# One-token decode block on one core: stationary values, 5p+k weights, wo by eight heads, feed-forward weights last

## The chip, the core and the metric

One NeuronCore of a Trainium2 chip runs the whole program. The metric is the device time of one execution in microseconds; the kernel before has a median of 693.3 us over three runs (693.24 to 693.9). A profile is one more execution, recorded instruction by instruction. In it PE is TensorE, PEld its weight loads, DVE VectorE, ACT ScalarE, POOL GpSimd, SP the engine that issues most transfers.

## The reference, cut to what matters

One token x of 640 features passes an attention block over a cache of 16,384 positions with 32 heads of 128, then a gated feed-forward of width 1,728. Both are modulated by six vectors made from c.

```python
mod = (silu(c) @ w_mod).reshape(1, 6, 1, 640)      # sa, ca, ga, sb, cb, gb
h = layernorm(x) * (1 + ca) + sa
q = (h @ wq) per head                              # 32 heads of 128
p = softmax(q . k_cache * 128 ** -0.5)             # 16384 scores a head
o = p . v_cache
x = x + ga * (o @ wo)
h = layernorm(x) * (1 + cb) + sb
x = x + gb * ((silu(h @ w_gate) * (h @ w_up)) @ w_down)
```

Everything is bf16. K and V are 32 x 4 MB each, 268 MB of the 290 MB that the core reads.

## The kernel before, in words

The kernel writes each engine's order out by hand. Every operation is given an engine, a position (a number that looks like a time in us) and the operations it depends on; each engine's operations are sorted by position (L91) and run in that order, waiting on semaphores. Positions are no delays: they only set the order on one engine. Nearly all transfers are issued by SP, whose order is therefore also the order of the transfers, and an SP issue that waits holds back all issues behind it.

**Layout.** In K and V a partition holds 128 consecutive positions, so that each partition's share of a head is one row of 32 KB. `kring` and `vring` hold two heads each. A vector of 640 features lies as 128 partitions by 5 columns with feature 128k+p in partition p, column k; c and x are read that way (L70), element by element. Weights follow: `(k p) n -> p k n`, so that a partition holds single rows of the matrix, and a stationary operand is a contiguous block of 128 columns.

**Start.** w_mod's first two vectors (L289), layernorm with two sums over partitions on GpSimd (L308, L316), then q for heads 0 to 3 (L338). The rest of wq takes the place of the first w_mod part and waits for it; its q products come later.

**A head.** ScalarE scales an identity by q (L402), PE multiplies it by ones so that q stands in every partition (L405), and ScalarE copies that to `qbc_sb` (L408). VectorE multiplies the whole K slot by q in place (L419), folds the 128 products of each position in halves: 128 to 64 out of the K slot into a buffer `f1` (L421), 64 to 32 and 32 to 16 in `f1` (L431), then sums 16 to one score (L433) and takes the maximum (L436). GpSimd takes the maximum over partitions (L439), ScalarE the exponential with its sum (L443), GpSimd the sum over partitions (L446). For values PE holds four columns of P stationary and streams V, 32 products of 512 columns (L458); the 4 x 512 result is copied (L464), its diagonal blocks are picked with eight small f32 matmuls (L470), scaled (L474), and multiplied at once by that head's 128 rows of wo (L481, five products).

**Loads of a head.** K(h) waits for the first fold of head h-2, V(h) for the value products of head h-2, the 160 KB of wo(h) for head h-2's wo products. On SP the order is K(h+1), V(h), wo(h-1) and so on. The last two V heads come in four pieces.

**End.** After V(31) SP loads the rest of w_mod into K slot 0, then w_gate, w_up and w_down into the weight region. The second layernorm (again two GpSimd sums) gives h; gate and up are one step of 140 products (L529) that waits for both weights; then the sigmoid and product on ScalarE and VectorE (L533 to L537), down in two steps, 60 and 10 products (L544), the gated residual (L549, L551), a transpose on PE (L553) and a copy (L554), so that the output is stored as five rows of 256 B.

Of the kernel before, what the change touches and what calls it, by code (L numbers as in the profile page):

```python
# [141 lines left out]
def build(nc, A_x, A_k, A_v, A_wq, A_wo, B_wg, B_wu, B_wd, c_in, w_mod, out, dbg=None, cfg=None):  # L142
    cfg = dict(cfg or {})
# [6 lines left out]
    FCH = (F + 127) // 128  # L150
    FLAST = F - 128 * (FCH - 1)
    NMOD = 6 * KC
    HB = min(cfg.get("HB", 4), H)
    assert H % HB == 0
    NQB = H // HB
    assert TT % 4 == 0
    NJ = TT // 4
    NFOLD = cfg.get("NFOLD", 3)
    SCALE = float(Dh) ** -0.5
    EPS = 1e-5  # L160
    PERIOD = 20.0
    T0 = 21.0
    NKP0 = 4 if TT % 16 == 0 else 1
    def NVP(h):
        return 4 if (h >= H - 2 and TT % 16 == 0) else 1

    es = ExitStack()
    with es:
        block = es.enter_context(nc.Block())
        plan = _Plan(nc, es)  # L170
        if cfg.get("names") is not None:
            plan.names = cfg["names"]

        def sb(name, shape, dtype):
            return es.enter_context(nc.sbuf_tensor(name, list(shape), dtype))

        ones_bf = sb("ones_bf", [128, 128], BF16)
        ident = sb("ident", [128, 128], BF16)
        c_col = sb("c_col", [128, KC], BF16)
        x_col = sb("x_col", [128, KC], BF16)  # L180
        LATE_MB = (TT * 128 >= KC * 4 * D) and H >= 3
        NA = 2 * KC
        WMA_E = KC * 2 * D
        WQ0_E = KC * HB * 128
        WQR_E = KC * (H - HB) * 128
        WMB_E = KC * 4 * D
        FFN_E = 2 * KC * F + FCH * D
        WREG_E = max(WMA_E + WQ0_E, WQR_E, FFN_E) + (0 if LATE_MB else WMB_E)
        wreg = sb("wreg", [128, WREG_E], BF16)
        wma_v = wreg[:, 0:WMA_E].rearrange("p (k n) -> p k n", k=KC)  # L190
        wq0_v = wreg[:, WMA_E:WMA_E + WQ0_E].rearrange("p (k n) -> p k n", k=KC)
        wqr_v = wreg[:, 0:WQR_E].rearrange("p (k n) -> p k n", k=KC) if H > HB else None
# [4 lines left out]
        if LATE_MB:  # L197
            wmb_v = kring[:, (H - 2) % 2].rearrange("p t d -> p (t d)")[:, 0:WMB_E].rearrange("p (k n) -> p k n", k=KC)
        else:
            wmb_v = wreg[:, WREG_E - WMB_E:WREG_E].rearrange("p (k n) -> p k n", k=KC)  # L200
        vring = sb("vring", [128, 2, TT, 128], BF16)
        f1 = sb("f1", [128, TT, 64], BF16)
        woring = sb("woring", [128, 2, D], BF16)
        S_sb = sb("S_sb", [128, 2, TT], F32)
        P_sb = sb("P_sb", [128, 2, TT], BF16)
        R_sb = sb("R_sb", [128, 2, 128], BF16)
        qbc_sb = sb("qbc_sb", [128, 2, 128], BF16)
        q_bf = sb("q_bf", [128, H], BF16)
        q_r32 = sb("q_r32", [128, H], F32)
# [7 lines left out]
        On = sb("On", [128, H], BF16)  # L217
        acc_sb = sb("acc_sb", [4, 2, 512], F32)
        onesf = sb("onesf", [4, 4], F32)
        identf = sb("identf", [4, 4], F32)  # L220
        mod_col = sb("mod_col", [128, NMOD], F32)
        onep = sb("onep", [128, 2, KC], F32)
# [5 lines left out]
        st = sb("st", [128, 16], F32)  # L228
        xc = sb("xc", [128, KC], F32)
        junk = sb("junk", [128, KC], F32)  # L230
# [5 lines left out]
        tt2 = sb("tt2", [128, KC], F32)  # L236
        h2_col = sb("h2_col", [128, KC], BF16)
# [5 lines left out]
        tt3 = sb("tt3", [128, KC], F32)  # L243
        o_col = sb("o_col", [128, KC], BF16)
        o_row = sb("o_row", [KC, 128], BF16)

        psb = [es.enter_context(nc.psum_tensor("psb%d" % i, [128, 512], F32)) for i in range(8)]
        qbc_ps = [psb[0][:, 0:128], psb[1][:, 0:128]]
# [3 lines left out]
        q_ps = psb[5]  # L252
        g_ps = psb[4]
        u_ps = psb[5]
        f_ps = psb[6]
        oT_ps = psb[7]
        acc_ps = [psb[6][0:4, :], psb[7][0:4, :]]
# [3 lines left out]

        o_ones = op(POOL, 0.0, lambda e: e.memset(ones_bf[:], 1.0), name="ones")
        o_ident = op(POOL, 0.1, lambda e: e.affine_select(
            out=ident[:], in_=ones_bf[:], pattern=[[1, 128]], compare_op=ALU.is_equal,
            fill=0.0, base=0, channel_multiplier=-1), deps=[o_ones], name="ident")

        o_onesf = op(POOL, 0.2, lambda e: e.memset(onesf[:], 1.0), name="onesf")
        o_identf = op(POOL, 0.3, lambda e: e.affine_select(
            out=identf[:], in_=onesf[:], pattern=[[1, 4]], compare_op=ALU.is_equal,
            fill=0.0, base=0, channel_multiplier=-1), deps=[o_onesf], name="identf")  # L270

        wm_src = w_mod.rearrange("(k p) n -> p k n", p=128)
        d_wm = plan.dma(0.0, wma_v, wm_src[:, :, 0:2 * D], "wm", name="dma_wmod_a")
        d_c = plan.dma(0.1, c_col[:], c_in[0].rearrange("(c p) -> p c", p=128), "c", noncontig=True, name="dma_c")
        d_x = plan.dma(0.15, x_col[:], A_x[0, 0].rearrange("(c p) -> p c", p=128), "x", noncontig=True, name="dma_x")
        wq_src = A_wq.rearrange("(k p) n -> p k n", p=128)
        d_wq0 = plan.dma(0.3, wq0_v, wq_src[:, :, 0:HB * 128], "wq0", name="dma_wq0")

        o_tbl = op(ACT, 0.0, lambda e: e.preload_act_table_set("natural_log_exp_and_others"), name="tbl")
# [5 lines left out]
        def f_mod(e, wv, j0, j1, jofs):  # L285
            last = None
            for j in range(j0, j1):
                for k in range(KC):
                    last = e.matmul(mod_ps[:, j:j + 1], lhsT=wv[:, k, 128 * (j - jofs):128 * (j - jofs + 1)], rhs=silu_c[:, k:k + 1],  # L289
                                    start=(k == 0), stop=(k == KC - 1))  # L290
            return last
        o_mod = op(PE, 1.0, lambda e: f_mod(e, wma_v, 0, NA, 0), deps=[d_wm, o_sc], name="mod_mm_a")
        o_modc_a = op(ACT, 1.5, lambda e: e.activation(out=mod_col[:, 0:NA], in_=mod_ps[:, 0:NA], func=ACTF.Copy), deps=[o_mod], name="mod_col_a")
        TLAST = T0 + (H - 1) * PERIOD
        if LATE_MB:
            TB = TLAST + 2.0
            TBC = TLAST + 41.5
        else:
            TB = T0 + 2 * PERIOD - 4.0
            TBC = min(TB + 2.5 * PERIOD, T0 + H * PERIOD - 8.0)  # L300
        mb_deps = [o_sc, o_modc_a]
        d_wm_b = None
        o_onep = op(DVE, 1.6, lambda e: e.tensor_scalar_add(out=onep[:, 0, :], in0=mod_col[:, KC:2 * KC], scalar1=1.0), deps=[o_modc_a], name="onep_a")
        o_onep_b_pos = TBC + 0.4

        def layernorm_ops(pos, src_f32, src_dep, rs_col, tag, xc_t, want_rs=None):
            c0 = rs_col
            o_tot = op(POOL, pos, lambda e: e.partition_all_reduce(  # L308
                st[:, c0 + 1:c0 + 2], st[:, c0:c0 + 1], channels=128, reduce_op=bass.bass_isa.ReduceOp.add),
                deps=[want_rs], name=tag + "_tot")  # L310
            o_xc = op(DVE, pos + 0.1, lambda e: e.tensor_scalar(
                out=xc_t[:], in0=src_f32[:], scalar1=float(D), scalar2=st[:, c0 + 1:c0 + 2], op0=ALU.mult, op1=ALU.subtract),
                deps=[o_tot, src_dep], name=tag + "_xc")
            o_sq = op(ACT, pos + 0.2, lambda e: e.activation(
                out=junk[:], in_=xc_t[:], func=ACTF.Square, accum_out=st[:, c0 + 2:c0 + 3]), deps=[o_xc], name=tag + "_sq")
            o_tot2 = op(POOL, pos + 0.3, lambda e: e.partition_all_reduce(  # L316
                st[:, c0 + 3:c0 + 4], st[:, c0 + 2:c0 + 3], channels=128, reduce_op=bass.bass_isa.ReduceOp.add),
                deps=[o_sq], name=tag + "_tot2")
            o_ln = op(ACT, pos + 0.4, lambda e: e.activation(
                out=st[:, c0 + 4:c0 + 5], in_=st[:, c0 + 3:c0 + 4], func=ACTF.Ln, scale=1.0 / float(D) ** 3, bias=EPS),  # L320
                deps=[o_tot2], name=tag + "_ln")
            o_rstd = op(ACT, pos + 0.5, lambda e: e.activation(
                out=st[:, c0 + 5:c0 + 6], in_=st[:, c0 + 4:c0 + 5], func=ACTF.Exp, scale=-0.5, bias=-math.log(float(D))),
                deps=[o_ln], name=tag + "_rstd")
            return o_xc, o_rstd

        o_xf = op(ACT, 0.3, lambda e: e.activation(out=x_f32[:], in_=x_col[:], func=ACTF.Copy, accum_out=st[:, 0:1]), deps=[d_x], name="x_f32")
        o_xc, o_rstd = layernorm_ops(0.6, x_f32, o_xf, 0, "ln1", xc, want_rs=o_xf)
        o_t1 = op(DVE, 1.7, lambda e: e.scalar_tensor_tensor(
            out=tt1[:], in0=xc[:], scalar=st[:, 5:6], in1=onep[:, 0, :], op0=ALU.mult, op1=ALU.mult),  # L330
            deps=[o_xc, o_rstd, o_onep], name="t1")
        o_h = op(DVE, 1.8, lambda e: e.tensor_tensor(out=h_col[:], in0=tt1[:], in1=mod_col[:, 0:KC], op=ALU.add), deps=[o_t1, o_modc_a], name="h_col")

        def f_q(e, wv, h0, h1):
            last = None
            for hh in range(h0, h1):
                for k in range(KC):
                    last = e.matmul(q_ps[:, hh:hh + 1], lhsT=wv[:, k, 128 * (hh - h0):128 * (hh - h0 + 1)], rhs=h_col[:, k:k + 1],  # L338
                                    start=(k == 0), stop=(k == KC - 1))
            return last  # L340
# [10 lines left out]
        if H > HB:  # L351
# [3 lines left out]
            for hh in range(HB, H):  # L355
                o_qr[hh] = o_qr1
# [272 lines left out]
```

## Time and profile before

| What | Value |
|---|---|
| median of the runs | 693.3 us (693.24 to 693.9) |
| profiled execution, first to last instruction (its span, and the only time recorded of it) | 692.7 us |
| busy: PE, DVE, ACT, POOL | 358.9, 618.7, 82.9, 255.5 us |
| bytes read | 290.47 MB, 419 GB/s over the span |
| packets of transfers | 22,176, of which 9,610 under 2 KB and 3,146 under 512 B |
| chain that ended last | DMA 62%, DVE 32%, issue 3% |
| first K multiply starts | 23.67 us |
| K load, issue to landing, median | 26.6 us |

The page cuts the span into 40 slices of 17.3 us and shows the busy share of each engine and of the 16 transfer engines in tenths. A group line gives line, engine, operation, shapes and count, then busy time, mean ns of one, idle time before it and what ended that. A row of the stretches gives the stretch, its length, the busy time and count of each engine, the granted TensorE clock, the share of the transfer engines and the rate. The chain is followed back from the last instruction: each step was released by the one before it.

### The profile page before, as it was taken

The numbers are of one execution on the slowest core, as the hardware profiler recorded it, in microseconds if no ns is written. First come the engines' busy times: TensorE is split into PE (matmuls) and PEld (weight loads), VectorE is DVE, ScalarE is ACT, GpSimd is POOL, SyncE is SP. The second block draws the span as 40 slices with busy tenths as digits, with TensorE's granted clock in tenths as the row PEclk, the third lists the DMA queues.
The fourth block names the chain that finished last, engine by engine and source line by source line (L and its number), as shares of the span: only waits on it lengthen the run. The fifth ranks groups of instructions, "written<-read, shape, count | busy, mean of one in ns | idle before, by whom it ended". The sixth has DMA issues, their size and how long they took to land.

```text
span 692.7 us, 4851 instructions
## 1 busy us (share of the span) xinstructions
PE 358.9 (52%) x1993; PEld 152.9 (22%) x1993; DVE 618.7 (89%) x220; ACT 82.9 (12%) x309; POOL 255.5 (37%) x76
## 2 busy tenths in 40 slices
PE   0025655444666544446555444566554446655665
PEld 0022212112222211122221212222121122221225
DVE  0699999999999999999999999899999999999911
ACT  1101101111011011111110111101011111110110
POOL 0043334444433344443334444023344443334400
PEclk9999767777666777766777776666677776677985
DMA  8999999999999999999999999999999999999995
GB/s 296 426 441 425 430 431 429 430 430 427 425 436 431 430 428 429 433 428 431 431 428 425 432 433 428 427 433 433 425 430 428 431 431 430 431 431 414 419 408 211
DMA packets 22176, 290.79 MB, mean 420 GB/s; under 512 B 3146, under 2 KB 9610, under 8 KB 12810
## 3 DMA queue, kind: packets, MB, share of 16 engines
q1 hardware_dynamic: 22154, 290.48, 98.9%
q8 instruction: 15, 0.25, 0.1%
q14 instruction: 7, 0.06, 0.0%
HBM read 290.47 MB, written 0.00 MB: 419 GB/s over the span
## 4 chain that ended last, share of the span: by engine, by line
DMA 62%; DVE 32%; issue 3%; SPq 1%; PE 1%; ACT 0%; POOL 0%; POOLq 0%; DVEq 0%
DMA kring<-in_A_k_cache_dram 58%; DVE kring L419 20%; DVE f L421 10%; DMA wreg<-in_B_w_up_dram 4%; SPq L71 1%; PE psb L529 1%; DVE f L431 1%; PE psb L544 0%; DVE S_sb L433 0%; PE psb L338 0%; ACT P_sb L443 0%; POOL st L308 0%; ACT R_sb L402 0%; POOL st L316 0%; POOL gm L439 0%
## 5 line engine op out<-in xcount | busy, mean ns | idle before, releaser
L458 PE MATMUL psb<-vring,P_sb 128*4 128x512 bf16 x1024 | 293.1, 456 | 10.6 <-DMA vring<-in_A_v_cache_dram 9.7
L419 DVE TENSOR_TENSOR kring<-kring,qbc_sb 128x16384 bf16<-128x16384 bf16 (+1 forms) x35 | 278.6, 7959 | 19.1 <-DMA kring<-in_A_k_cache_dram 16.6
L446 POOL PARTITION_ALL_REDUCE Ls<-rs x32 | 233.5, 7295 | 34.8 <-ACT P_sb L443 34.8
L439 POOL PARTITION_ALL_REDUCE gm<-pm x32 | 19.6, 612 | 354.8 <-DVE pm L436 344.2
L421 DVE TENSOR_TENSOR f<-kring 128x8192 bf16<-128x8192 bf16 (+1 forms) x35 | 142.1, 4059 | 1.2
L458 PEld LDWEIGHTS psb<-vring,P_sb 128*4 128x4 bf16 x1024 | 97.1, 98 | 194.0 <-issue 96.6
L405 PE MATMUL psb<-R_sb,ones_bf 128*128 128x128 bf16 x32 | 9.2, 288 | 235.8 <-ACT R_sb L402 235.8
L431 DVE TENSOR_TENSOR f<-f 128x4096 bf16<-128x4096 bf16 x64 | 112.5, 1758 | 2.2
L433 DVE TENSOR_REDUCE S_sb<-f 128x128 f32<-128x2048 bf16 x32 | 73.1, 2286 | 1.1
L405 PEld LDWEIGHTS psb<-R_sb,ones_bf 128*128 128x128 bf16 x32 | 3.3, 104 | 238.7 <-ACT R_sb L402 238.7
L464 ACT ACTIVATE acc_sb<-psb 4x512 f32<-4x512 f32 x32 | 18.8, 586 | 284.7 <-PE psb L458 284.7
L470 PE MATMUL psb<-identf,acc_sb 4*128 4x1 f32 x256 | 33.5, 248 | 21.6 <-ACT acc_sb L464 21.6
L470 PEld LDWEIGHTS psb<-identf,acc_sb 4*128 4x128 f32 x256 | 30.8, 186 | 37.8 <-ACT acc_sb L464 37.8
L448 ACT ACTIVATE lnl<-Ls 128x1 f32<-128x1 f32 x32 | 6.5, 203 | 221.7 <-POOL Ls L446 221.7
L338 PE MATMUL psb<-h_col,wreg 128*128 128x1 bf16 x160 | 4.6, 165 | 28.6 <-DMA wreg<-in_A_wq_dram 18.0
L481 PE MATMUL psb<-On,woring 128*128 128x1 bf16 x160 | 8.9, 166 | 19.7 <-ACT On L474 19.7
L491 DVE TENSOR_SCALAR onep<-mod_col 128x5 f32<-128x5 f32 x1 | 0.2, 169 | 16.2 <-ACT mod_col L490 16.2
L443 ACT ACTIVATE P_sb<-S_sb,nb 128x128 bf16<-128x128 f32 x32 | 12.9, 402 | 1.0
L402 ACT ACTIVATE R_sb<-ident,q_r 128x128 bf16<-128x128 bf16 x32 | 12.4, 387 | 0.0
L481 PEld LDWEIGHTS psb<-On,woring 128*128 128x128 bf16 x160 | 6.1, 97 | 22.4 <-ACT On L474 22.4
L338 PEld LDWEIGHTS psb<-h_col,wreg 128*128 128x128 bf16 x160 | 4.4, 104 | 28.8 <-DMA wreg<-in_A_wq_dram 18.2
L408 ACT ACTIVATE qbc_sb<-psb 128x128 bf16<-128x128 f32 x32 | 8.9, 277 | 12.2 <-PE psb L405 12.2
(61 smaller groups left out, 70.7 us busy)
## 6 DMA issues: line engine op xcount, KB each, us to landing
kring<-in_A_k_cache_dram SPq DMA_DIRECT2D x31, 4096.0 KB, 26.6
vring<-in_A_v_cache_dram SPq DMA_DIRECT2D x30, 4096.0 KB, 30.4
vring<-in_A_v_cache_dram SPq DMA_DIRECT2D x8, 1024.0 KB, 22.1
woring<-in_A_wo_dram SPq DMA_DIRECT2D x32, 160.0 KB, 28.4
wreg<-in_A_wq_dram SPq DMA_DIRECT2D x1, 4480.0 KB, 20.1
kring<-in_A_k_cache_dram SPq DMA_DIRECT2D x4, 1024.0 KB, 10.3
kring<-in_w_mod_dram SPq DMA_DIRECT2D x1, 3200.0 KB, 27.1
wreg<-in_B_w_gate_dram SPq DMA_DIRECT2D x1, 2160.0 KB, 31.9
```

The source lines that it names most:

```text
L405: o_qbcmm[h] = op(PE, base - 14.8 if h > 0 else 2.7, lambda e, s2=s2: e.matmul(qbc_ps[s2], lhsT=ones_bf[:], rhs=R_sb[:, s2], start=True, s ...
L419: o_m = op(DVE, base + 3.3 * c, lambda e, ksl=ksl, qb=qb: e.tensor_tensor(out=ksl, in0=ksl, in1=qb, op=ALU.mult), deps=[d_k[h][c], o_qbc[h ...
L421: o_f = op(DVE, base + 3.3 * c + 2.2 + (6.6 if npc == 1 else 0.0), lambda e, ksl=ksl, c=c, KP=KP: e.tensor_tensor(out=f1[:, c * KP:(c + 1) ...
L431: prev = op(DVE, base + 13.3 + i, lambda e, w=w: e.tensor_tensor(out=f1[:, :, 0:w], in0=f1[:, :, 0:w], in1=f1[:, :, w:2 * w], op=ALU.add), ...
L433: o_red[h] = op(DVE, base + 17.0, lambda e, w=w, s2=s2: e.tensor_reduce(out=S_sb[:, s2], in_=f1[:, :, 0:w], axis=AX.X, op=ALU.add), deps=[ ...
L439: o_gm[h] = op(POOL, base + 19.6, lambda e, h=h: e.partition_all_reduce(gm[:, h:h + 1], pm[:, h:h + 1], channels=128, reduce_op=bass.bass_ ...
L443: o_exp[h] = op(ACT, base + 20.4, lambda e, h=h, s2=s2: e.activation(out=P_sb[:, s2], in_=S_sb[:, s2], func=ACTF.Exp, scale=SCALE, bias=nb ...
L446: o_L[h] = op(POOL, base + 21.0, lambda e, h=h: e.partition_all_reduce(Ls[:, h:h + 1], rs[:, h:h + 1], channels=128, reduce_op=bass.bass_i ...
L458: last = e.matmul(acc_ps[s2], lhsT=P_sb[:, s2, 4 * j:4 * j + 4], rhs=vring[:, s2, 4 * j:4 * j + 4, :].rearrange("p a d -> p (a d)"), start ...
L464: o_acc[h] = op(ACT, base + 39.5, lambda e, s2=s2: e.activation(out=acc_sb[:, s2, :], in_=acc_ps[s2], func=ACTF.Copy), deps=[o_pvlast[h], ...
L470: last = e.matmul(OT_ps[:, h:h + 1], lhsT=acc_sb[:, s2, 128 * i:128 * (i + 1)], rhs=identf[:, i:i + 1], start=(i == 0), stop=(i == 3))
L481: last = e.matmul(attn_ps[:, cc:cc + 1], lhsT=woring[:, s2, 128 * cc:128 * (cc + 1)], rhs=On[:, h:h + 1], start=(h == 0 and cc == 0), stop ...
```

## The change

It is a rewrite of most of `build`; the planner is the same.

- **Feature 5p+k.** Partition p, column k now hold feature 5p+k. Every weight is read `(p k) n -> p k n`, so that a partition holds five consecutive rows, and c, x and the output are 10 contiguous bytes a partition. Stationary operands then step through the matrix: by 5 elements in w_mod, wo and w_down, by 13 in gate and up (feature 13p+k of the 1,664 that fill 13 columns; the last 64 are as before). The transpose at the end goes.
- **c and x** are issued by ScalarE, ahead of its table load; all others by SP.
- **Sums over partitions** of the layernorms are PE products with f32 ones instead of GpSimd reductions. GpSimd has one warm-up reduction.
- **q** is broadcast by the matmul itself: h is the stationary operand, its column repeated 128 times, and wq is streamed, 512 columns at a time. `qbc` keeps all heads. wq has a place of its own.
- **Folds in place.** `f1` goes: all folds write into the K slot, which becomes free at the reduction (L422 of the new kernel) instead of the first fold. K(h+1) is issued ahead of V(h), as it was.
- **Values stationary.** Each 128 x 128 block of V is loaded as weights and multiplied by one column of P, 128 products a head, which gives the output as a column; no diagonal.
- **wo by eight heads.** wo is read in four loads of 1.3 MB, eight consecutive rows a partition (10,240 B). The eight head outputs are put through a masked copy and one small matmul to the layout that this needs, then 40 products.
- **The end.** V(30) whole, the rest of w_mod, V(31) in halves, then w_gate, w_up and w_down in three pieces. Gate and up are two steps that wait for their own weights; down has three.

SP's order is now: w_mod's first part, wq of heads 0 to 3, K(0) in quarters, K(1), V(0), the rest of wq, wo, K(2), V(1), K(3), V(2), and so on.

```diff
-            d_wo[h] = plan.dma(base + 1.5, woring[:, s2], A_wo[h * 128:(h + 1) * 128, :], ("wo", s2),
+            if h % GW == 0:
+                d_wo[g8] = plan.dma(base + 13.0, wo_sb[:], A_wo[g8 * GW * 128:(g8 + 1) * GW * 128, :].rearrange("(p k) n -> p k n", p=128),
+                                    "wo", deps=[o_wo[g8 - 1]] if g8 else [], name="dma_wo%d" % g8)
...
-            kdeps = [o_fold1[h - 2]] if h >= 2 else []
+            deps = [o_red[h - 2]] if h >= 2 else []
...
+        d_c = plan.dma(0.0, c_col[:], c_in[0].rearrange("(p k) -> p k", p=128), "c", name="dma_c", eng="act")
...
+            o_tot = op(PE, pos, lambda e: e.matmul(st_ps[:, c0:c0 + 1], lhsT=ones_f[:], rhs=sum_ap, start=True, stop=True),
...
+                        last = e.matmul(mod_ps[:, m * KC + k:m * KC + k + 1],
+                                        lhsT=wv[:, kd, (m - m0) * D + k:(m - m0 + 1) * D:KC], rhs=silu_c[:, kd:kd + 1],
...
+                    last = e.matmul(q_ps[b][:, 0:n * 128], lhsT=h_col[:, k:k + 1].broadcast_to([128, 128]),
+                                    rhs=wv[:, k, n0:n0 + n * 128], start=(k == 0), stop=(k == KC - 1))
...
-                    out=f1[:, c * KP:(c + 1) * KP, :], in0=ksl[:, :, 0:64], in1=ksl[:, :, 64:128], op=ALU.add),
+                    out=ksl[:, :, 0:64], in0=ksl[:, :, 0:64], in1=ksl[:, :, 64:128], op=ALU.add),
...
-                        last = e.matmul(acc_ps[s2], lhsT=P_sb[:, s2, 4 * j:4 * j + 4],
-                                        rhs=vring[:, s2, 4 * j:4 * j + 4, :].rearrange("p a d -> p (a d)"),
+                        last = e.matmul(OT_ps[:, h:h + 1], lhsT=vring[:, s2, t, :], rhs=P_sb[:, s2, t:t + 1],
+                                        start=(t == 0), stop=(t == TT - 1))
...
+                out=Z[:, zb, JW * hl:JW * (hl + 1)], in_=msk[:], func=ACTF.Copy, scale=on_f[:, h:h + 1]),
+                o_am[g8] = op(PE, base + 29.4, lambda e, zb=zb: e.matmul(A_ps[:, 0:GW], lhsT=Z[:, zb], rhs=e8[:], start=True, stop=True),
+                            last = e.matmul(attn_ps[:, cc:cc + 1], lhsT=wo_sb[:, k, cc:D:KC], rhs=A_sb[:, zb, k:k + 1],
...
+                        last = e.matmul(ps_t[:, j:j + 1], lhsT=wv[:, k, j:128 * NF:NF], rhs=h2_col[:, k:k + 1],
+        o_g = op(PE, TE + 1.2, lambda e: f_gu(e, wg_v, g_ps), deps=[o_h2, d_wg, o_zg], name="gate")
+        o_u = op(PE, TE + 1.25, lambda e: f_gu(e, wu_v, u_ps), deps=[o_h2, d_wu, o_zu], name="up")
+                        last = e.matmul(f_ps[:, cc:cc + 1], lhsT=wd_v[0:kw, k, cc:D:KC], rhs=gu_col[0:kw, k:k + 1],
```

## The prediction

> **What bounds the kernel now.** I read the page's 40 slices first, then the costliest groups, then busy time by stretch, and last the chain that ended last.
>
> ```profile
> DMA  8999999999999999999999999999999999999995
> GB/s 296 426 441 425 430 431 429 430 430 427 425 436 431 430 428 429 433 428 431 431 428 425 432 433 428 427 433 433 425 430 428 431 431 430 431 431 414 419 408 211
> ```
>
> The transfers are busy in every slice. 290 MB go by at about 430 GB/s; only the first slice (296) and the last four (414, 419, 408, 211) fall below. So time can be won at the two ends, or by bytes that move faster, and hardly by less compute in the middle. The second limit is close:
>
> ```profile
> L419 DVE TENSOR_TENSOR kring<-kring,qbc_sb 128x16384 bf16<-128x16384 bf16 (+1 forms) x35 | 278.6, 7959 | 19.1 <-DMA kring<-in_A_k_cache_dram 16.6
> ...
> L421 DVE TENSOR_TENSOR f<-kring 128x8192 bf16<-128x8192 bf16 (+1 forms) x35 | 142.1, 4059 | 1.2
> ...
> L431 DVE TENSOR_TENSOR f<-f 128x4096 bf16<-128x4096 bf16 x64 | 112.5, 1758 | 2.2
> L433 DVE TENSOR_REDUCE S_sb<-f 128x128 f32<-128x2048 bf16 x32 | 73.1, 2286 | 1.1
> ```
>
> By the groups with shapes kept apart, VectorE's head is 8.69 + 4.42 + 2.29 + 1.23 + 2.29 + 0.29 = 19.2 us, 19.4 with handovers (621.70 to 641.08 in the timeline). Multiplies start 19.9 us apart (601.82, 621.70, 641.61), with 0.5 us of waiting for K. A head moves 8.55 MB, 19.9 us at 430. Transfers set the pace and VectorE follows half a microsecond behind.
>
> The stretches show the ends (us; busy time and count of PE, PEld, DVE, ACT, POOL; granted clock; DMA share; GB/s):
>
> ```profile
> 7.00:8.00 1.00, 0.00 (x0) 0.00 (x0) 0.00 (x0) 0.00 (x0) 0.00 (x0) 1.00 0.41 14
> 8.00:9.00 1.00, 0.00 (x0) 0.00 (x0) 0.36 (x2) 0.21 (x1) 0.00 (x0) 1.00 0.34 37
> 400.00:500.00 100.00, 54.51 (x224) 21.48 (x223) 95.14 (x31) 12.16 (x45) 34.31 (x10) 0.68 1.01 430
> 670.00:678.00 8.00, 5.83 (x122) 4.34 (x121) 0.48 (x5) 1.11 (x4) 0.12 (x1) 0.87 1.03 405
> 680.00:683.00 3.00, 1.62 (x61) 1.65 (x62) 0.31 (x2) 0.00 (x0) 0.00 (x0) 0.50 1.06 363
> 686.00:687.00 1.00, 0.05 (x1) 0.05 (x2) 0.76 (x4) 0.00 (x0) 0.00 (x0) 0.50 0.16 55
> 687.00:688.00 1.00, 1.00 (x39) 1.00 (x40) 0.00 (x0) 0.00 (x0) 0.00 (x0) 0.50 0.00 0
> ```
>
> From 7 to 9 us the share is 0.41 and 0.34 and only 51 KB move: that is where c and x come in 1,280 pieces of 2 bytes. At 670 to 678 (gate and up, rows of 3,456 B) a full share yields 405 GB/s, at 680 to 683 (w_down, rows of 1,280 B) 363. The last bytes land near 686.5. What follows is in the chain:
>
> ```profile
> 681.38 4.42 PE psb L529 x140
> ...
> 686.95 1.77 PE psb L544 x60
> 688.73 0.05 issue
> 688.77 1.25 PE psb L544 x10
> ...
> 690.77 0.27 ACT o_row L554
> ```
>
> All 140 gate and up products wait for w_up (landed 681.24), so down begins at 686.95, after the bytes are in: 6.2 us from the last byte to the span's end.
>
> **The change, part by part.** The sum is made against the span, 692.7 us; the median of the runs is 693.3, so I add 0.6 at the end.
>
> *Transfers.* Bytes stay, pieces grow. (1) c and x: 256 pieces of 10 B on ScalarE's queue beside w_mod. The hole is 2.0 us long for 0.1 us of work; a fifth of the pieces takes a fifth of its busy share (0.75 us): 0.2. Won: 1.7. (2) wo: 5.24 MB in rows of 1,280 B, priced by w_down's row (363): 14.4 us; in 10,240 B pieces near 425: 12.3. I take 2.0, with 0 as the lower bound, since no row has wo alone. (3) gate and up: 4.42 MB, 10.9 us at 405 against 10.3 at 428: 0.6. (4) w_down: 2.21 MB, 6.1 against 5.3 (most pieces 11,520 and 5,120 B): 0.8. (5) V(30) whole and V(31) in halves instead of quarters: 417 GB/s from 641 to 661 against 430, 8.4 MB: 0.5. Sum 5.6: the last byte lands at 680.9.
>
> [...]
>
> *The last bytes.* Gate now waits for w_gate alone, up for w_up, and w_down is three steps, the last of 64 rows. After the last byte come 5 products of 64 rows (0.18 each in the by-form groups, 0.9), two VectorE steps (0.4 with handovers), the store (691.04 to 692.7: 1.66; transpose and copy, 0.6 us, go, 128 pieces instead of 5 may cost 0.2): 3.1 instead of 6.2. Won: 3.1.
>
> *Is TensorE then late?* V(31) now comes after w_mod's second part, and the feed-forward weights (6.6 MB, 15.5 us) after that; its last half lands near 665. Then: 64 value products 2.0 (31 ns each, as gate's 140 in 4.40); head output, masked copy, small matmul, copy and 40 wo products 2.4; residual 0.65 (L507 to L510); layernorm 2.9 (677.61 to 680.35 today, two GpSimd sums of 0.38 become f32 matmuls of about 0.5 by L470's 0.19 load and 0.25 product); gate and up 4.4; gu 0.2; down 2.9; end 2.2. Sum 17.6: 682.6 on this path against 680.9 + 3.1 = 684.0 on the transfers'. Slack 1.4.
>
> *Strided weights.* With feature 5p+k, the stationary operands of w_mod, wo and w_down step by 5 elements and those of gate and up by 13. The trace has no such load. Bounds: nothing (contiguous bf16, 31 ns a pair) and 100 ns more, the f32 load of L470 (8 pairs in 1.05 us, 131 ns). The nearest row, same type and size, is the contiguous one; I take nothing, keep both ends. On the path stand 250 of them (40 + 140 + 70): each extra ns is 0.25 us, the first 5 ns are free.
>
> [...]
>
> *Values stationary.* 128 pairs of 31 ns, 4.0 us a head for 9.2 (L458, 293.1 over 32), and the 4-row copy and diagonal products go. PE was not the bound: nothing, except that V slots free earlier.
>
> *K slot freed later.* K(h+2) now waits for the reduction instead of the first fold: 2.29 + 1.23 + 2.29 and handovers, 5.9 us later; the order K(h+1), V(h) on SP stays. Cover: K lands 26.6 us after issue, 9.7 of them its own, so 17 us stand ahead; 11 remain. Cost nothing; with the cover gone each us late is lost per head. The V load queued behind it on SP waits no longer than K.
>
> *In-place folds.* Same counts; only the row pitch is 256 B instead of 128. L419 and L431 are in place already. Nothing; bounds are in the rivals. Without wo a head's transfers take 8.39 MB / 431 = 19.5 us against VectorE's 19.4, so VectorE nearly ties, with 11 us of queue as buffer.
>
> *Start.* Sums move from GpSimd (its first waits until 18.53) to PE, and the first multiply from 23.67 to about 12.5, when K(0)'s first quarter lands. Nothing won: K(1), V(0), wq, wo fill the queue to about 51, and K(2), free at 32, is late next. The seven q evictions stand on ScalarE ahead of head 1's exp and wait for wq (about 50); only head 1's value product and V(3) wait for that, 20 us later.
>
> Sum: 692.7 − 5.6 − 3.1 = 684.0, plus 0.6: **684.6 us**.
>
> **Rivals.** *Slow strided loads, slower side.* One mechanism: PE's 250 loads after V(31). At L470's 100 ns extra: 682.6 + 25 = 707.6, 708.2 as a median. It decides beyond 5 ns and loses to before beyond (692.7 − 682.6) / 0.25 = 40 ns. For: 2-byte steps break the contiguous pattern of every load seen. Against: same type and size as the 31 ns rows. *Half rate*, 27 ns more on all: 689.4, 690.0 as a median; on gate and up alone 687. *Pieces bring nothing*: if 363 and 405 come from the queue running out, only the tail is won: 692.7 − 3.1 + 0.6 = 690.2. For: the share falls to 0.16 at the very end. Against: 670 to 678 is mid-queue at 1.03. *VectorE becomes the bound*: if the 256 B pitch costs the folds and reduction 10% (1.0 us of 10.2), 32 us build up, less 11 of queue, 21 on 684.6: 706. Against: L431's 32-element runs already run at L421's rate.
>
> **How the numbers follow.** Forecast 0.50 (681 to 686.5); half rate 0.18 (686 to 692); pieces bring nothing 0.12 (688 to 691.5); slow loads over 40 ns 0.12; VectorE 0.05; near no change 0.03. Two tenths of a percent (1.4 us) is about what a measurement here can tell. Faster 0.50 + 0.17 + 0.12 = 0.79, same 0.04, slower 0.17. The range 681 to 692 holds the first three, 0.80; its lower end has the engines' uneven finish (share 0.64 to 0.16, about 2 us) gone, its upper end the half rate.
>
> **What would show it.** After: no stretch below 0.9 of DMA share from 3 us to the end; wo's heads no slower than others; last byte near 681; a chain that ends with w_down's landing and ten or fewer products. Gate's 70 products should take 2.2 us; 5 or more means strided loads cost. I am wrong if the chain's end is PE, or VectorE waits for nothing between heads.

## The result and the profile after

The changed kernel takes 698.0 us (median of four runs, 697.32 to 699.3) against 693.27 (four runs, 693.17 to 693.9). The ratio is 1.0067, with an interval of 1.0053 to 1.0082: slower by 4.7 us, where 684.6 was predicted and 681 to 692 given as the range. The profiled execution took 697.41 us with a span of 695.7.

The page of the changed kernel: its span, the 40 slices of the transfers, one row of the queues, and groups.

```profile
span 695.7 us, 10154 instructions
...
DMA  8999999999999999999999999999999999999992
GB/s 320 447 411 439 431 433 427 433 430 431 432 420 434 431 432 430 432 429 431 434 423 434 429 430 433 429 429 436 427 425 432 430 436 429 427 434 432 405 424 90
...
q8 instruction: 36, 0.59, 0.3%
...
L412 DVE TENSOR_TENSOR kring<-kring 128x8192 bf16<-128x8192 bf16 (+1 forms) x35 | 142.1, 4059 | 1.2
...
L525 PE MATMUL psb<-h_col,wreg 128*128 128x1 bf16 x130 | 8.1, 199 | 1.0 <-DVE h_col L513 1.0
...
L474 PE MATMUL psb<-A_sb,wo_sb 128*128 128x1 bf16 x160 | 7.2, 179 | 1.6 <-ACT A_sb L467 1.1
```

The middle is as forecast: 430 GB/s a slice, and VectorE's folds cost to the nanosecond what they did. What differs is at the end. Slice 39 moves 424 GB/s instead of 408, but slice 40 only 90 instead of 211: few bytes are left for it, and the kernel still has 17 us to go. Two rows were not looked for beforehand. The 130 gate and up products with step 13 take 8.1 us, 62 ns each, where 31 had been taken. And the row "q8 instruction", a queue that the program does not issue, has 36 packets. Before, these rows were:

```profile
span 692.7 us, 4851 instructions
...
q8 instruction: 15, 0.25, 0.1%
```

The program has 5,303 more instructions: the 128 loads and 128 products a head that replace 32 wide pairs add 6,144, and the rest of the rewrite saves some 800. The page counts the time of the queue called "instruction", 0.3% against 0.1% before, as a share of the 16 transfer engines' span; in an experiment below, each of its packets goes with one of a transfer's 16 increments coming 1.4 to 1.7 us later.

The chain of the changed kernel that ended last (start, length in us, what):

```profile
643.66 27.33 DMA vring<-in_A_v_cache_dram
...
671.04 1.88 PE psb L450 x64
...
674.05 1.77 PE psb L474 x40
...
679.29 4.06 PE psb L525 x65
683.35 0.35 PE psb L528 x5
683.70 4.00 PE psb L525 x65
687.71 0.37 PE psb L528 x5
...
688.40 1.97 PE psb L546 x45
...
692.15 0.17 DVE o_col L552
```

The chain is no longer the transfer of the last weights but TensorE's path: V(31)'s second half lands at 670.99, and from there it is one step after the other to 692.3, when the store is issued (L71, 692.35). The span ends at 695.7. Between rows that are left out stand small steps of ScalarE and VectorE.

The changed kernel by stretches (the columns are those of the prediction's table):

```profile
679.00:680.00 1.00, 0.71 (x12) 0.72 (x13) 0.20 (x2) 0.00 (x0) 0.00 (x0) 0.50 0.56 233
...
682.00:683.00 1.00, 1.00 (x20) 1.00 (x20) 0.00 (x0) 0.00 (x0) 0.00 (x0) 0.50 0.51 218
...
685.00:686.00 1.00, 1.00 (x19) 1.00 (x19) 0.00 (x0) 0.00 (x0) 0.00 (x0) 0.50 0.28 92
686.00:687.00 1.00, 1.00 (x20) 1.00 (x19) 0.00 (x0) 0.00 (x0) 0.00 (x0) 0.50 0.01 4
```

TensorE is full from 680 on and does some 20 pairs in a microsecond. Before, at the same granted clock of 0.50, it did 43 in the same phase:

```profile
682.00:683.00 1.00, 1.00 (x43) 1.00 (x41) 0.00 (x0) 0.00 (x0) 0.00 (x0) 0.50 1.07 361
```

The transfer share stands near one half from 679 to 685 (0.50 in the mean): as if some engines had finished and others had not. So I read landings by the trace's 16 increments of one transfer, as many as there are transfer engines, and take each for one engine's finish. Of the last piece of w_down eight come at 678.5 to 680.7 and eight at 685.2 to 686.8. First, median and last, in us:

| Transfer | before | changed kernel |
|---|---|---|
| K(31) | 638.0, 639.9, 641.6 | 634.9, 639.5, 643.4 |
| V(31), second half | (in quarters) | median 666.9, last 671.0 |
| last piece of w_down | 683.6, 685.9, 687.2 | 678.5, 683.0, 686.8 |

At the median engine the last bytes arrive 2.9 us earlier than before, at the slowest 0.4. A step that needs a transfer starts behind the last increment: V(31)'s products at 671.04, after 670.99, and before, gate and up at 681.38, after w_up's 681.24.

### The profile page after: what moved, and what is told of

It reads as the page before. It is cut to its first block, busy times and chain, and to the rows that moved or that the text cites. A ratio compares the mean times of both kernels' runs of the same rounds, so it can differ in the third digit from the quotient of the medians.

```text
span 695.7 us, 10154 instructions
## 1 busy us (share of the span) xinstructions
PE 155.3 (22%) x4672; PEld 144.7 (21%) x4673; DVE 619.3 (89%) x224; ACT 62.7 (9%) x252; POOL 286.7 (41%) x71
## 4 chain that ended last, share of the span: by engine, by line
DMA 53%; DVE 41%; PE 3%; issue 1%; SPq 0%; ACT 0%; DVEq 0%
DMA kring<-in_A_k_cache_dram 45%; DVE kring L410 19%; DVE kring L412 10%; DMA vring<-in_A_v_cache_dram 8%; DVE kring L419 8%; DVE S_sb L422 5%; PE psb L525 1%; PE psb L450 1%; PE psb L474 1%; PE psb L546 0%; SPq L71 0%; PE psb L528 0%; ACT Z L460 0%; PE psb L285 0%; PE psb L278 0%
## 5 line engine op out<-in xcount | busy, mean ns | idle before, releaser
L410 DVE TENSOR_TENSOR kring<-kring,qbc 128x16384 bf16<-128x16384 bf16 (+1 forms) x35 | 278.6, 7961 | 30.5 <-DMA kring<-in_A_k_cache_dram 29.6
L428 POOL PARTITION_ALL_REDUCE gm<-pm x32 | 121.9, 3808 | 323.6 <-DVE pm L425 323.6
L450 PE MATMUL psb<-P_sb,vring 128*128 128x1 bf16 x4096 | 115.6, 165 | 511.8 <-DMA vring<-in_A_v_cache_dram 469.2
L450 PEld LDWEIGHTS psb<-P_sb,vring 128*128 128x128 bf16 x4096 | 112.9, 104 | 515.6 <-ACT P_sb L432 188.1
L435 POOL PARTITION_ALL_REDUCE Ls<-rs x32 | 163.0, 5093 | 34.4 <-ACT P_sb L432 34.4
L412 DVE TENSOR_TENSOR kring<-kring 128x8192 bf16<-128x8192 bf16 (+1 forms) x35 | 142.1, 4059 | 1.2
L419 DVE TENSOR_TENSOR kring<-kring 128x4096 bf16<-128x4096 bf16 x64 | 112.5, 1758 | 2.2
L422 DVE TENSOR_REDUCE S_sb<-kring 128x128 f32<-128x2048 bf16 x32 | 73.1, 2286 | 1.1
L327 PE MATMUL psb<-wreg,h_col 128*128 128x512 bf16 (+2 forms) x44 | 11.1, 422 | 9.0 <-DMA wreg<-in_A_wq_dram 9.0
L460 ACT ACTIVATE Z<-msk,on_f 128x16 bf16<-128x16 f32 x32 | 9.8, 308 | 1.0
L504 DVE TENSOR_TENSOR tt<-attn_bf,modb 128x5 f32<-128x5 bf16 x1 | 0.2, 166 | 10.2 <-ACT attn_bf L503 10.2
```

Source lines behind the costliest of these rows:

```text
L327: last = e.matmul(q_ps[b][:, 0:n * 128], lhsT=h_col[:, k:k + 1].broadcast_to([128, 128]), rhs=wv[:, k, n0:n0 + n * 128], start=(k == 0), s ...
L410: o_m = op(DVE, base + 3.3 * c, lambda e, ksl=ksl, qb=qb: e.tensor_tensor(out=ksl, in0=ksl, in1=qb, op=ALU.mult), deps=[d_k[h][c], o_qbc[h ...
L412: fd.append(op(DVE, base + 3.3 * c + 2.2 + (6.6 if npc == 1 else 0.0), lambda e, ksl=ksl: e.tensor_tensor(out=ksl[:, :, 0:64], in0=ksl[:, ...
L419: prev = [op(DVE, base + 15.5 + 1.5 * i, lambda e, kslot=kslot, w=w: e.tensor_tensor(out=kslot[:, :, 0:w], in0=kslot[:, :, 0:w], in1=kslot ...
L422: o_red[h] = op(DVE, base + 18.2, lambda e, s2=s2, kslot=kslot, w=w: e.tensor_reduce(out=S_sb[:, s2], in_=kslot[:, :, 0:w], axis=AX.X, op= ...
L428: o_gm = op(POOL, base + 19.0, lambda e, h=h: e.partition_all_reduce(gm[:, h:h + 1], pm[:, h:h + 1], channels=128, reduce_op=bass.bass_isa ...
```

## The experiments

Two theories stood at first. **Strided loads:** the price of a stationary operand that steps by 5 or 13 elements explains the loss, and the rest went as forecast. **The longer program:** the 5,303 more instructions, and with them the 36 packets of 16 KB on the queue "instruction" instead of 15, cost transfer time, unevenly over the engines. All runs were compared with the kernel before on the same chip: it took 693.46 to 693.69 us there. The changed kernel itself was not run on these chips; a difference from its 698.0 us given below may be off by 0.4 us for that reason, besides the spread of its runs (697.32 to 699.3).

### Gate and up contiguous

```diff
-        wd_src = B_wd[0:128 * NF, :].rearrange("(p k) n -> p k n", p=128)
+        wd_src = B_wd[0:128 * NF, :].rearrange("(k p) n -> p k n", p=128)
...
-                        last = e.matmul(ps_t[:, j:j + 1], lhsT=wv[:, k, j:128 * NF:NF], rhs=h2_col[:, k:k + 1],
+                        last = e.matmul(ps_t[:, j:j + 1], lhsT=wv[:, k, 128 * j:128 * (j + 1)], rhs=h2_col[:, k:k + 1],
```

> The changed kernel with gate and up taking 128 neighbouring columns as stationary operand (feature 128j+p) instead of every 13th; w_down's rows are read to match (row 128k+p, pieces of 1,280 B again). Theory A (strided loads on TensorE after V(31) set the end): the 130 full loads fall from 8.1 us to about 3.6, so the end comes 4.4 us earlier, near 693.5, unless the transfers' end becomes the bound. Theory B (the late landing of V(31) and of the weights sets the end, and PE only follows): under 1 us, near 697.5. w_down's smaller pieces cost up to 0.8 us of transfer under either.

Measured: 696.39 us, 1.0038 (1.0023 to 1.0053), 1.6 us less than the changed kernel. The group with shapes kept apart, and then the end of the chain, of this kernel:

```profile
L525 PE MATMUL psb<-h_col,wreg 128*128 128x1 bf16 x130 | 3.8, 165 | 1.0 <-DVE h_col L513 1.0
```

```profile
649.37 35.90 DMA wreg<-in_B_w_down_dram
685.27 0.14 issue
685.41 1.95 PE psb L546 x45
```

The 130 products fall from 8.1 to 3.8 us, so the stride costs 4.3 us on TensorE: shown. But only 1.6 of it reach the end, between what the two theories forecast. Down now starts at 685.41 instead of 688.40, held up by w_down's first piece, which lands at 685.27 (684.7 in the changed kernel, where its rows are longer). And the store, issued at 689.33, needs until 694.6: 5.2 us to the end of the span instead of 3.3. Strided loads are a cause, but not the whole: behind them stood a late landing, and a store that now takes longer.

### Values moving again, all else as changed

Heads 0 to 30 get back the 32 products of 512 columns, the copy and the diagonal; head 31 stays as changed.

```diff
-            for c in range(nvp):
+            for c in range(nvp if h == H - 1 else 0):
...
+                    for j in range(TT // 4):
+                        last = e.matmul(f_ps[0:4, :], lhsT=P_sb[:, s2, 4 * j:4 * j + 4],
+                                        rhs=vring[:, s2, 4 * j:4 * j + 4, :].rearrange("p a d -> p (a d)"),
+                                        start=(j == 0), stop=(j == TT // 4 - 1))
```

> The changed kernel with the value products of heads 0 to 30 in the old form (P stationary, V streamed 512 columns at a time, diagonal by eight small products); head 31 stays as changed, so the end's own work is the same. TensorE has about 5,000 instructions fewer. Theory C (the longer program is fetched through some of the transfer engines, these fall behind, and every load lands with its slowest engine): the spread of the 16 landings of a late K load falls from 8.5 us to about 3.5, V(31) lands 3 to 4 us earlier, the time falls to about 694 and the gap between median and span shrinks from 1.8 to about 0.7 us. Rival D (the spread comes from the larger pieces or from the tighter K slot): spread and time stay, 697 to 698.5.

Measured: 694.62 us, 1.0011 (1.0002 to 1.0021), 3.4 us less than the changed kernel, although TensorE is busy for 361.6 us instead of 155.3. Its page:

```profile
span 693.1 us, 4733 instructions
...
q8 instruction: 15, 0.25, 0.1%
```

The queue of instructions is back at 15 packets. V(31)'s second half lands at 668.2 instead of 671.0, K(31) spreads over 636.7, 637.9, 640.8, the last w_down piece over 679.5, 681.1, 683.8. For that piece the median and the last engine are now 2.7 us apart instead of 3.8. That the time outside the span would shrink with the program was wrong: it is 1.75 us, as everywhere.

### The kernel before with a longer program, and controls

```diff
+            if h < H - 1:
+                def f_extra(e):
+                    last = None
+                    for i in range(86):
+                        last = e.matmul(mod_ps[:, 64:65], lhsT=ones_bf[:], rhs=ones_bf[:, 0:1], start=True, stop=True, skip_group_check=True)
+                    return last
+                op(PE, base + 41.1, f_extra, deps=[o_ones], name="extra%d" % h)
```

> The kernel before with 86 extra products of one column (contiguous ones, into an unused PSUM column) after each of the first 31 heads: 5,332 more instructions on TensorE, nothing else, and some 2.5 us of PE time a head that PE has to spare. Theory C: the spread of landings of a late K load grows from 3.5 us to about 8, the last weights land 3 to 4 us later, the time grows to about 697, and median minus span from 0.6 to about 1.8 us. Rival D: the time stays within 0.5 us of 693.3.

Measured: 698.41 us, 1.0069 (1.0054 to 1.0084), the same loss as the change's, with 36 packets on the queue of instructions. But the 86 products of head 30 are 2.29 us of TensorE's time just ahead of the last values, so the cause was not yet isolated. Controls followed. The first has few instructions and much work, ten products of 384 columns after each of the same heads:

```diff
+                    for i in range(10):
+                        last = e.matmul(psb[0][:, 128:512], lhsT=ones_bf[:], rhs=ones_bf[:].unsqueeze(1).broadcast_to([128, 3, 128]), start=True, stop=True, skip_group_check=True)
```

> Control for the kernel before with 5,332 more instructions: at the same place, 10 products of 384 columns a head instead of 86 of one column, about the same TensorE time, but 620 more instructions instead of 5,332. Theory C (the fetch of the longer program): landings stay as in the kernel before (spread about 3.5 us) and the time stays within 1 us of 693.7. Rival F (the extra TensorE work itself, ahead of the last head's values, or its reads): 696 to 698.4.

Measured: 695.16 us, 1.0022 (1.0013 to 1.0031). Its transfers land as before's do (K(31) at 636.9, 639.0, 640.8), so its 1.7 us, between the two forecasts, can come from the 3.22 us of TensorE's work ahead of the last values, which was not tested by itself. With 4,712 instructions more, the kernel with the many products is 3.25 us slower than this control. A pair of kernels without that doubt leaves the last heads alone: 95 one-column products after heads 0 to 27 against 11 products of 384 columns after the same heads.

```diff
+            if h < H - 4:
...
+                    for i in range(95):
```

> The kernel before with 95 extra products of one column after each of heads 0 to 27 (5,320 more instructions), none near the end, so that the last heads' TensorE path is as before. Theory C: the last landings come 3 to 3.5 us later than before as with 86 a head (slowest w_up near 684.7), the end follows: 3 to 3.5 us, 696.7 to 697. If the slower time of the earlier run was the extra TensorE work ahead of the last values: no change, 693.5.

```diff
+            if h < H - 4:
...
+                    for i in range(11):
```

> Its control: 11 products of 384 columns after each of heads 0 to 27 (616 more instructions, the same TensorE time or more), none near the end. Theory C: within 0.5 us of the kernel before, with landings as before. Rival (TensorE's reads slow the transfers or VectorE): 695 or more.

Measured: 699.24 us, 1.0085 (1.0063 to 1.0107), with the many; 694.39, 1.0008 (0.9999 to 1.0017), with the wide ones. The medians differ by 4.85 us. The four runs with the many lie between 697.93 and 700.73, so this number is good to about 1.5 us; the two profiled executions differ by 3.8. The pages of the two, the many first:

```profile
span 696.2 us, 10171 instructions
...
q8 instruction: 36, 0.59, 0.3%
```

```profile
span 692.4 us, 5467 instructions
...
q8 instruction: 18, 0.29, 0.2%
```

And from the chain of the kernel with the many, then of its control:

```profile
656.49 28.29 DMA wreg<-in_B_w_up_dram
684.77 0.14 issue
684.91 4.43 PE psb L536 x140
```

```profile
652.15 28.30 DMA wreg<-in_B_w_up_dram
```

It is the chain of before, step for step, with w_up landing at 684.77; in the control it lands at 680.45, before at 681.24. The extra products end four heads before the end, on an engine that has time (it is busy for 428 of 696 us, 423 in the control), and add no bytes of the program's own. So **4,704 more instructions cost this kernel, which is bound by transfers, some 4 to 5 us**, as much as the whole loss of the change. The 18 additional packets of 16 KB are 0.3 MB, 0.7 us at 430 GB/s; the landing is 4.3 us late at the slowest engine. K(31) lands 637.2, 641.3, 645.2 against the control's 637.1, 639.1, 640.8: the load is not spread evenly.

The increments and the queue's packets in the trace of the kernel with the many show how it is spread. Each packet takes 0.9 to 1.1 us, and each makes one more engine late:

| Packets of that queue before the landing | engines on time (us) | engines late (us) |
|---|---|---|
| none | 16 at 40.9 to 41.4 | none |
| 1 (starts at 45.5) | 15 at 50.7 to 51.2 | 1 at 52.5 |
| 2 (62.8) | 14 at 70.5 to 71.0 | 2 at 72.2 and 72.3 |
| 3 (80.4) | 13 at 80.7 to 81.2 | 3 at 82.3 to 82.6 |
| 4 (99.4) | 12 at 100.5 to 100.9 | 4 at 102.2 to 102.6 |
| 34, w_up's landing | 8 at 676.7 to 679.0 | 8 at 682.9 to 684.8 |

By this reading the packets go in turn to eight of the 16 engines, and each holds its engine back by 1.4 to 1.7 us (the difference of the two columns' means, for each packet). In the kernel before it is the ninth packet that makes one engine late a second time: after eight, the increments of K(20) come at 419.3 to 421.4, after nine those of K(21) at 439.2 to 441.3, but the last at 442.7. The 34 before w_up lands are four or five for each of the eight, the control's 15 about two: three more on the slowest engine are an estimated 4 to 5 us, beside the 4.3 measured. The 0.7 us had spread the bytes over all 16 engines at the full rate; both were wrong for these packets.

### The price of a step

The whole computation is left out; only 128 load and product pairs for each step run, in two passes.

```diff
+        s5 = op("pe", 1.0 + 0.1 * 5, lambda e: many(e, lambda e, i: e.matmul(ps[:, 5:6], lhsT=w[:, 0:640:5], rhs=x[:, 0:1], start=(i == 0), stop=(i == 127))), deps=[o_w, o_x], name="s5")
```

> A probe that leaves out the reference's whole computation: TensorE alone runs 26 bursts of 128 products with 128 x 128 stationary operands whose columns step by 1, 1, 2, 3, 4, 5, 6, 7, 8, 13, 16, 32, 64 elements of bf16, twice over, one moving column, no transfers beside it. In the changed kernel a pair takes 28 ns at step 1, 43 at 5, 61 at 13. [...] Rival A2 (two levels, below and beyond 8 elements): 43 from 2 to 7, 61 from 8 on. Rival A3 (the difference came from contention with transfers): all about 28.

Measured, by groups with shapes kept apart, costliest first. Lines L161, L163, L164, L165, L168, L169, L172 have steps 1, 3, 4, 5, 8, 13, 64; the first number behind the bar is the busy time of 128 pairs in us.

```profile
L172 PE MATMUL ps<-x,w 128*128 128x1 bf16 x128 | 11.7, 229 | 0.0
...
L169 PE MATMUL ps<-x,w 128*128 128x1 bf16 x128 | 7.9, 199 | 0.0
...
L168 PE MATMUL ps<-x,w 128*128 128x1 bf16 x128 | 7.8, 198 | 0.0
...
L165 PE MATMUL ps<-x,w 128*128 128x1 bf16 x128 | 5.3, 178 | 0.0
L164 PE MATMUL ps<-x,w 128*128 128x1 bf16 x128 | 4.4, 172 | 0.0
...
L163 PE MATMUL ps<-x,w 128*128 128x1 bf16 x128 | 3.6, 165 | 0.0
...
L161 PE MATMUL ps<-x,w 128*128 128x1 bf16 x128 | 3.6, 165 | 0.0
```

Divided by 128 a pair takes 27.7 ns up to step 3, then 34, 41, 48, 54 for 4, 5, 6, 7, and 59 to 65 from 8 to 32; with 64 it is 91. (The third number is the mean length of one product, in ns; neighbours overlap, so the price is busy time over count.) Rivals A2 and A3 are out. From step 3 to step 8 the price rises evenly, by about 6.7 ns a step, and it stays within 59 to 65 up to 32. Why steps 2 and 3 cost nothing more, why the rise ends at 8 and why 64 is dearer again, no run shows. The granted clock was 1.00 here and 0.50 where the changed kernel does gate and up, and step 13 takes 62 ns in both: the lower clock did not make these loads slow.

### Values moving and gate and up contiguous together

> The two undone parts together on the changed kernel: values of heads 0 to 30 with V streamed (5,000 instructions fewer), gate and up with neighbouring columns. If both causes are real and add: V(31) lands near 668 as with the first alone, gate and up take 4.4 us instead of 8.8, then down waits for w_down (slowest engine near 684) and the end is 5 us after that: span 689.4, time 691.1, faster than both kernels. If one of them only uncovers the other's wait: no better than 694.6.

The edits are those of the first two experiments. Measured: 693.76 us, 1.0002 (0.9993 to 1.0011), no change, where 691.1 had been expected. Its last w_down piece lands at 679.8, 681.8, 682.8, its last product ends at 685.1 and the store is issued at 685.56, yet the span ends at 690.9. The store's row of this kernel, and that of the changed kernel (KB, us from issue to landing):

```profile
out_dram<-o_col SPq DMA_DIRECT2D x1, 1.2 KB, 5.0
...
out_dram<-o_col SPq DMA_DIRECT2D x1, 1.2 KB, 2.9
```

The store of 128 pieces of 10 B takes 5.0 us here, 4.8 in the kernel with gate and up contiguous, 2.8 with values moving, and 2.9 in the changed one. In all four the packets themselves are over 1.0 to 1.1 us after the issue; what differs is the time from there to the increments. The two slow stores come 2.2 and 2.8 us after the last landing of w_down, the two quick ones 5.6 and 6.1 us after it, but only the slow ones also have gate and up contiguous; which of the two counts was not tested.

### And the output as one row

Five products bring o_col into one partition (0.71 us), two copies side by side follow (1.22), and the store is one piece of 1,280 B.

```diff
-        d_out = plan.dma(TE + 2.3, out[0, 0].rearrange("(p k) -> p k", p=128), o_col[:], "out", deps=[o_oc], name="dma_out")
+                last = e.matmul(orow_ps[k // 3][0:1, (k % 3) * 128:(k % 3 + 1) * 128], lhsT=o_col[:, k:k + 1], rhs=ident[:], start=True, stop=True, skip_group_check=True)
...
+        d_out = plan.dma(TE + 2.3, out[0], o_row, "out", deps=[o_r0, o_r1], name="dma_out")
```

> The kernel of the combination, and the output put into one row of 640 by five small products and two copies, then stored as one piece of 1,280 B instead of 128 pieces of 10 B. Theory E (small pieces make the store slow: 3.35 us from its issue to the end in the changed kernel against 1.6 in the one before): the store takes 1.6 us, the products and copies 0.9: 0.8 us less than without it. Rival: the store's time is the write's latency whatever the pieces: 0.9 us more.

Measured: **691.78 us, 0.9976 (0.9967 to 0.9985)**, faster than both kernels. The end of its chain:

```profile
646.32 35.97 DMA wreg<-in_B_w_down_dram
682.29 0.14 issue
682.43 1.95 PE psb L576 x45
...
686.38 0.71 PE psb L586 x5
687.09 0.02 issue
687.11 1.22 ACT acc_sb L592
```

The store is issued at 688.35 and the span ends at 689.9: 1.5 us instead of 5.4. Two microseconds of extra work win two at the end. How much of that comes from the one large piece is not fully separated: this store also comes 4.0 us after the last weights instead of 2.8. Beside the quickest stores of 10-byte pieces, 3.2 us from issue to end, the one piece still wins 1.6. From 698.0 us, the shorter program alone took off 3.4, contiguous gate and up alone 1.6, both 4.2, and the store a further 2.0.

### c and x issued by SP again

```diff
-        d_c = plan.dma(0.0, c_col[:], c_in[0].rearrange("(p k) -> p k", p=128), "c", name="dma_c", eng="act")
+        d_c = plan.dma(0.01, c_col[:], c_in[0].rearrange("(p k) -> p k", p=128), "c", name="dma_c")
```

(and x likewise)

> The changed kernel with c and x issued by SyncE after w_mod's first part, as before, instead of by ScalarE; pieces of 10 B stay. In the changed kernel the 16 landings of wq's first part spread over 2.5 us, before over 0.9. If the second queue makes the early spread: it falls to 1 us. If it is the absence of the pause (before, the engines caught up while c and x came in): it stays near 2.5 us and the time near 698.

Measured once: 697.88 us beside the changed kernel's 698.0. The first part of wq lands at 9.7, 10.0, 12.3, against 9.3, 10.2, 11.8 in the changed kernel. The engines' early spread, about 2.5 us, is not made by the second queue. What makes it stays open.

## Why the prediction was wrong, by its own steps

**Transfers, 5.6 us: the size nearly held, and a term was missing.** With the program short again (values moving), the median engine's last byte lands at 681.1, 4.8 us before the 685.9 of before, and 0.2 from the forecast's 680.9 (up to 1 us of the 4.8 may be that the profile of before was a late one, as said under the base below). At the slowest engine it is 3.4 (687.2 to 683.8). The longer program takes 1.9 of it at the median (683.0) and 3.0 at the slowest engine (683.8 to 686.8). The page had the clue: a row "q8 instruction" with 15 packets for 4,851 instructions, a number that the change doubles. The step "128 pairs, PE was not the bound: nothing" looked at TensorE's time alone. Of the parts, the start won 1.0 instead of 1.7 at the median engine (wq's first part 11.2 to 10.2) and nothing at the slowest. The other parts were not tried one by one.

**The last bytes, 3.1 us: wrong.** Two errors. "The last byte" was one moment for 16 engines, and even in the kernel before the slowest was done at 687.2, not 686.5. The share of 0.5 from 679 to 685 goes with the increments of w_down's last piece, eight by 680.7 and eight from 685.2, and the step behind a piece starts at its last increment. So the pieces of w_down come nearly together: even in the best version the first lands at 682.29 and all three steps stand behind it, not five products. And the store was put at 1.66 us plus 0.2 from its issue to the end; it took 3.3 in the changed kernel and up to 5.4 in the others with 10-byte pieces.

**TensorE's path, 17.6 us from 665: this is what set the end, at 24.7 us from 671.0.** The terms:

| Step | predicted | measured |
|---|---|---|
| V(31) lands | 665 | 671.0 |
| 64 value products | 2.0 | 1.9 |
| head output to wo | 2.4 | 2.9 |
| residual, layernorm | 3.55 | 3.4 |
| gate and up | 4.4 | 8.8 |
| gu | 0.2 | 0.3 |
| down | 2.9 | 3.55 |
| end and store | 2.2 | 3.8 |

Of the 13.1 us, 6.0 are the landing, 5.5 strided loads and 1.6 the store. Of the landing, 2.8 go with the longer program (668.2 without); nearly all of the other 3.2 is the engines' uneven finish, for in that kernel the median engine has V(31) at 665.3, the forecast's 665. The slack of 1.4 us that the prediction found was real and far too small for three such errors.

**Strided weights, taken at nothing: the failed choice.** The bounds (0 to 100 ns) held: beside 27.7 ns for a contiguous pair, step 5 costs 13 more and step 13 costs 34 more. The rule "the nearest row of same type and size" chose the contiguous one, though the very thing that was new was the pattern. The rival "half rate", 27 ns more on every load, came nearest: 13 for the 110 loads with step 5 and 34 for the 130 with step 13 are 23 on average over its 250. It gave only 690.0 because the landing and the store were wrong with it.

**The base, +0.6.** In most runs listed with both numbers, time less span is 1.7 to 1.8 us (before: 693.44 and 691.7). The profiled execution of before, with a span of 692.7, was thus probably one about a microsecond above the median; the 0.6 took that off again, but the moments worked out from it (665, 680.9) may be up to 1 us late for a usual run. That is not what failed.

**Right:** the in-place folds (142.1 and 112.5 us as before), the K slot's later release (the rate stays at 430), the values on TensorE by their own time, layernorm at 2.8, and the first multiply earlier (23.67 to 14.26, where 12.5 was forecast) with nothing won by it. The mean granted clock fell from 0.75 to 0.55, which the prediction did not speak of. Of the signs named beforehand one came as named, a chain whose end is PE; the other, gate's 70 products at 5 us or more, was set too high, for they took 4.4, twice the 2.2, and that was enough.

**What stays open.** Why a packet of 16 KB on the queue of instructions takes about as long as a K packet of 32 KB (0.9 to 1.1 us, and 1.2); the early spread of 2.5 us; why the store of 10-byte pieces takes 2.9 in one kernel and 5.0 in another; and a pause of 1.2 us inside the up products of the kernel with both edits (679.45, put down to "issue"). Five such pauses of 0.5 us or more, in the three kernels with values moving, end 1.2 to 1.4 us after a packet of the instruction queue does (this one at 680.65, after 679.30); whether the two belong together, no run tests.

## What to carry to other kernels

Where transfers set the pace, count a change's instructions as transfers: the row of the instruction queue and the instruction count stand for them, and here a thousand more cost 0.6 to 1 us (3.4 us for 5,421, 3.25 for 4,712, 4.85 for 4,704). Read a landing at the slowest of the engines, not at the mean rate (w_down's last piece: 686.8 at the slowest, 683.0 at the median), and price the path behind it step by step as the second bound. The layout that made the pieces of the loads from memory larger here moved the stride into TensorE's loads (a pair at 62 ns with step 13, 27.7 without) and the small pieces into the store (3.3 us from issue to end with 128 pieces, 1.66 with five before); price both before taking such a layout, by a small kernel that measures only them.

## What the runs showed of the hardware that was not expected

- Without transfers beside it, a load and one-column product cost 27.7 ns a pair for column steps 1 to 3 in bf16, 34 to 54 for 4 to 7, about 61 for 8 to 16, 91 for 64.
- 4,704 more instructions on an engine with time to spare cost 4.85 us in a kernel bound by transfers; the queue of instructions went from 18 to 36 packets.
- By the landings, these packets went in turn to eight of the 16 transfer engines, and each held its engine back by 1.4 to 1.7 us (kernel with 95 extra products a head).
- The 16 increments of one transfer arrive 3.6 us apart (K(31), before) and 8.5 in the changed kernel.
- A store of 128 pieces of 10 B took 3.2 to 5.4 us from its issue to the end of the span; one piece of 1,280 B took 1.5.
